# More key chunks summed on VectorE, and a layernorm that divides where v is split, in capped attention followed by a spatial gate

## The chip, the core and the metric

One core of a Trainium2 chip runs the kernel in one launch. The metric is the device time in microseconds (us). TensorE (PE) multiplies matrices, VectorE (DVE) and ScalarE (ACT) work on elements, GpSimd (POOL) does a few integer adds and powers, and SyncE (SP) issues the DMAs.

## The reference

Four batches of twelve heads, 448 positions, head size 64; a model width of 768 and a hidden width of 1024.

```python
scores = cap * np.tanh(scale * (q @ k.T) / cap)
attn = np.exp(scores - max); attn = attn / (np.sum(attn, axis=-1, keepdims=True) + 1e-09)
x = heads side by side of attn @ v                     # (4, 448, 768)
h = gelu_tanh(x @ w_in)                                # (4, 448, 1024)
u, v = h[..., :512], h[..., 512:]
mu = np.mean(v, axis=-1, keepdims=True); var = np.mean((v - mu) ** 2, axis=-1, keepdims=True)
v_n = (v - mu) / np.sqrt(var + 1e-06) * g_ln
v_s = np.einsum('ts,bsd->btd', w_sg, v_n) + b_sg[None, :, None]
return x + (u * v_s) @ w_out
```

## The kernel before

Attention works on two heads (a pair) at a time and on two pairs (a group) together; a batch has three groups, the kernel twelve. The keys of a pair lie in chunks of 128, the last 64 keys of both pairs in one common tail chunk, so a group has seven units: chunks 1 to 3 of either pair and the tail (chunk 0). Per unit there is a score matmul (three products of high and low parts, or one in whole fp32 where PLAIN says so), a tanh and an exp on ScalarE (`tanh`, `exp`, lines 591 and 593), and a value matmul (line 552). The denominators need the sum over all keys of the exponentials. They are made by a matmul with ones (`sum`, line 451), and two units share one such operation. `SUMS` says for each group how much is summed ahead on VectorE (`add`, line 604): with 0 every unit goes to the ones matmul (seven units), with 1 the chunks 2 and 3 are added into chunk 1 of their pair (three units: two pairs and the tail), with 2 the tail is added too, each half of its partitions into its own pair (two units).

After the third group of a batch the denominators go through DRAM, are inverted and come back as rows; the gate of a batch (`gated`) then multiplies x by them, splits x in high and low parts, and multiplies by `w_in` (`hv` for v, line 725, and `hu` for u, line 763), three matmuls for each product. `hv` ends in gelu and layernorm on a tile of 128 positions by 512: statistics, mean, an added epsilon, a power of -0.5 on GpSimd (line 739), centering and scaling in one instruction on VectorE (line 741), then a copy (`v hi`) and a subtraction (`v lo`) that split it. `vsg` (line 780) multiplies by the spatial weights, `bias` and `gate` follow, and `outp` (line 800) multiplies by `w_out`. Matmuls of the gate of one batch run between those of the attention of the next ones.

The weights come as 64-bit floats and are decoded on the chip, 20 pieces of them: a low and a high multiply (lines 376 to 382), a shift, a sign, an integer add on GpSimd (line 396), and a split in high and low (lines 297 and 325). The scaling of q and k (`qk hi`, line 502, and `qk lo`, line 509) splits them likewise.

Nothing is scheduled at run time. Each step is an operation with a number and one or two engines that can do it, and `ORDER` lists them: the number is half of the entry, and an odd entry takes the second engine, which is ScalarE where both are offered. Every engine works through its part of the list in that order, and DMA issues wait in the SP queue in theirs. Buffers are taken from pools when the list comes to an operation: five tiles for exponentials (`p`), two score tiles in PSUM (`sc`).

Of the kernel before, what the change touches and what calls it, by code (L numbers as in the profile page):

```python
# [8 lines left out]
FP32 = mybir.dt.float32  # L9
# [19 lines left out]
SUMS = (0, 1, 1, 1, 0, 1, 1, 1, 2, 2, 2, 2)  # L29
# [87 lines left out]
)  # L117


# [98 lines left out]
def kernel(  # L218
# [13 lines left out]
    nc = tc.nc  # L232
# [668 lines left out]
```

## Time and profile before

| what | value |
|---|---|
| median of 3 runs | 377.6 us (376.75 to 378.32) |
| profiled execution | 376.92 us |
| its span, first to last instruction | 375.1 us |
| busy PE / DVE / ACT / POOL | 370.3 / 301.3 / 211.3 / 40.0 us |

The span lies 1.8 us below the time of its own execution. Matmuls are pipelined and their ends are modelled, so a busy PE can hide a short wait.

### The profile page before, as it was taken

The numbers are of one execution on the slowest core, as the hardware profiler recorded it, in microseconds if no ns is written. First come the engines' busy times: TensorE is split into PE (matmuls) and PEld (weight loads), VectorE is DVE, ScalarE is ACT, GpSimd is POOL, SyncE is SP. The second block draws the span as 40 slices with busy tenths as digits, with TensorE's granted clock in tenths as the row PEclk, the third lists the DMA queues.
The fourth block names the chain that finished last, engine by engine and source line by source line (L and its number), as shares of the span: only waits on it lengthen the run. The fifth ranks groups of instructions, "written<-read, shape, count | busy, mean of one in ns | idle before, by whom it ended". The sixth has DMA issues, their size and how long they took to land.

```text
span 375.1 us, 5508 instructions
## 1 busy us (share of the span) xinstructions
PE 370.3 (99%) x2064; PEld 251.9 (67%) x2064; DVE 301.3 (80%) x559; ACT 211.3 (56%) x275; POOL 40.0 (11%) x39
## 2 busy tenths in 40 slices
PE   9999999999999999999999999999999999999995
PEld 4334343455877497546478976486889999889995
DVE  2799999999999999989894779779276988438763
ACT  5999999995685758697914377751031411033200
POOL 0231121510310312030000100000001000001000
PEclk9999999999999999999999999999999999999999
DMA  7898264454371244146520022202120101400004
GB/s 262 290 285 280 91 187 151 118 158 150 98 255 44 65 135 172 43 134 201 150 80 2 20 73 46 76 3 78 36 74 24 47 5 50 171 2 0 2 0 171
DMA packets 23130, 39.65 MB, mean 106 GB/s; under 512 B 5472, under 2 KB 17728, under 8 KB 23104
## 3 DMA queue, kind: packets, MB, share of 16 engines
q1 hardware_dynamic: 22816, 38.96, 33.0%
q8 instruction: 16, 0.26, 0.3%
q10 hardware_dynamic: 288, 0.34, 0.3%
q14 instruction: 10, 0.08, 0.1%
HBM read 33.28 MB, written 6.02 MB: 105 GB/s over the span
## 4 chain that ended last, share of the span: by engine, by line
PE 96%; DVE 2%; ACT 1%; issue 0%; DVEq 0%; ACTq 0%
PE ps L552 15%; PE ps L725 13%; PE ps L763 13%; PE sc L520 11%; PE ps L800 10%; PE ps L780 9%; PE sc L800 6%; PE den L451 5%; PE sc L528 3%; PE sc L763 3%; PE ps L562 3%; PE sc L725 2%; PE sc L536 2%; PE sc L780 1%; PE ps L352 1%; DVE p L604 1%
## 5 line engine op out<-in xcount | busy, mean ns | idle before, releaser
L593 ACT ACTIVATE p<-p,cap 128x896 f32<-128x896 f32 x84 | 84.8, 1041 | 0.7
L591 ACT ACTIVATE p<-sc 128x896 f32<-128x896 f32 x63 | 56.4, 911 | 15.7 <-PE sc L520 6.9
L552 PE MATMUL ps<-p,v 128*64 128x448 f32 x288 | 61.3, 551 | 0.0
L604 DVE TENSOR_TENSOR p<-p,p 128x896 f32<-128x896 f32 (+1 forms) x48 | 53.8, 1130 | 5.5 <-PE ps L552 3.0
L725 PE MATMUL ps<-win,rg 128*128 128x512 f32 x205 | 50.3, 391 | 0.0
L763 PE MATMUL ps<-rg,win 128*128 128x448 f32 x223 | 50.3, 366 | 0.0
L520 PEld LDWEIGHTS sc<-hl 64*128 64x128 f32 x378 | 32.7, 184 | 25.6 <-ACT p L591 11.7
L520 PE MATMUL sc<-hl 64*128 64x448 f32 x378 | 48.3, 383 | 0.0
L763 PEld LDWEIGHTS ps<-rg,win 128*128 128x128 f32 x223 | 41.8, 188 | 4.4 <-issue 0.7
L725 PEld LDWEIGHTS ps<-win,rg 128*128 128x128 f32 x205 | 38.4, 188 | 8.3 <-issue 0.7
L396 POOL TENSOR_TENSOR stage<-stage 128x512 int32<-128x512 int32 (+1 forms) x20 | 30.6, 1532 | 113.4 <-DVE stage L391 58.1
L552 PEld LDWEIGHTS ps<-p,v 128*64 128x64 f32 x288 | 17.5, 136 | 34.1 <-issue 22.0
L706 ACT ACTIVATE t<-ps 128x448 f32<-128x448 f32 (+1 forms) x25 | 14.2, 567 | 46.4 <-PE ps L725 29.3
L800 PE MATMUL ps<-rg,wout 128*128 128x448 f32 x166 | 39.7, 368 | 0.0
L800 PEld LDWEIGHTS ps<-rg,wout 128*128 128x128 f32 x166 | 30.9, 188 | 5.3 <-issue 2.7
L780 PE MATMUL ps<-wsg,rg 128*128 128x448 f32 x130 | 30.6, 369 | 0.0
L711 ACT ACTIVATE t<-t 128x448 f32<-128x448 f32 (+1 forms) x30 | 18.0, 602 | 20.6 <-DVE t L708 20.6
L739 POOL TENSOR_TENSOR sm<-sm,pw 128x1 f32<-128x1 f32 x14 | 8.7, 627 | 186.7 <-DVE sm L737 177.9
L708 DVE SCALAR_TENSOR_TENSOR t<-t,ps 128x448 f32<-128x448 f32 (+1 forms) x25 | 16.2, 647 | 13.3 <-ACT t L706 13.3
L780 PEld LDWEIGHTS ps<-wsg,rg 128*128 128x128 f32 x130 | 24.0, 188 | 4.1 <-issue 1.0
L800 PE MATMUL sc<-rg,wout 128*128 128x448 f32 x98 | 24.3, 365 | 0.0
L591 ACT ACTIVATE p<-sc,qsc 128x896 f32<-128x896 f32 x21 | 21.0, 1005 | 5.4 <-PE sc L536 1.9
(115 smaller groups left out, 468.2 us busy)
## 6 DMA issues: line engine op xcount, KB each, us to landing
raw<-in_qk_dram SPq DMA_DIRECT2D x22, 448.0 KB
stage<-in_w_in_dram SPq DMA_DIRECT2D x12, 512.0 KB
n<-spread SPq DMA_DIRECT2D x24, 224.0 KB
out_dram<-x SPq DMA_DIRECT2D x23, 224.0 KB
v<-in_vp_dram SPq DMA_DIRECT2D x24, 192.0 KB
stage<-in_w_out_dram SPq DMA_DIRECT2D x8, 384.0 KB
u<-in_w_sgT_dram SPq DMA_DIRECT2D x4, 224.0 KB
vt<-in_vt_dram SPq DMA_DIRECT2D x12, 64.0 KB
```

The lines of the kernel that those rows point to most:

```text
L396: nc.gpsimd.tensor_tensor(out=a.bitcast(I32), in0=a.bitcast(I32), in1=hi, op=ALU.add)
L451: nc.tensor.matmul(out=den.t[32 * j:32 * j + 32, :S], lhsT=ones_sb[:, kind, NP - 1 - kind - p:NP + 31 - kind - p], rhs=src.t[:, h, :], sta ...
L520: nc.tensor.matmul(out=sc.t[:, h, :S], lhsT=hl[s].t[rows, w, 1, 128 * c - 128:128 * c], rhs=hl[s].t[rows, m, 0], start=(k == 0), stop=(k = ...
L552: nc.tensor.matmul(out=pav[s].t[64 * h:64 * h + 64, :S], lhsT=v[s].t[:, 128 * (c - 1) + 64 * h:128 * (c - 1) + 64 * h + 64], rhs=p.t[:, h, ...
L591: op(name("tanh", s, c), "act", c_act(2 * S, True, raw_scores), lambda p=p, sc=sc, r=raw_scores: nc.scalar.activation(out=p.t, in_=sc.t[:, ...
L593: op(name("exp", s, c), "act", c_act(2 * S, False, True), lambda p=p: nc.scalar.activation(out=p.t, in_=p.t, func=ACTF.Exp, scale=cap_sb), ...
L604: op(name("add", s, t), "dve", c_tt(2 * S), lambda: nc.vector.tensor_tensor(out=a.t[rows], in0=a.t[rows], in1=p.t[rows], op=ALU.add), rd=[ ...
L711: op(tag + " tanh", "act", c_act(n), lambda: nc.scalar.activation(out=view(), in_=view(), func=ACTF.Tanh, scale=GELU_C * GELU_A), wr=[sq])
L725: nc.tensor.matmul(out=ps.t[:, :HF], lhsT=(xl if a else xh)[c].t[:, t * 128:t * 128 + 128], rhs=win[w][:, c, HF:], start=(c == 0 and k == ...
L763: nc.tensor.matmul(out=ps.t[:, :S], lhsT=win[w][:, c, f * 128:(f + 1) * 128], rhs=(xl if a else xh)[c].t[:, :S], start=(c == 0 and k == 0) ...
L780: nc.tensor.matmul(out=ps.t[:, :S], lhsT=(vl if a else vh)[c].t[:, f * 128:(f + 1) * 128], rhs=wsg[w][:, c, :], start=(c == 0 and k == 0), ...
L800: nc.tensor.matmul(out=ps.t[:, :S], lhsT=wout[w][:, f, c * 128:(c + 1) * 128], rhs=(gl if a else gh)[f].t[:, :S], start=(f == 0 and k == 0 ...
```

## The change

`SUMS` changes for four groups: the fifth from 0 to 1, the sixth to the eighth from 1 to 2. The layernorm instruction now only centers, with the sign turned, and may run on either engine; it waits for the mean alone. The division by the deviation moves into the copy (a multiply by a column, on either engine) and the subtraction (one instruction that multiplies and subtracts) which split v. The turned sign is taken back by negated gains, `gneg`, one new instruction. The high multiply of the weight decoding may run on ScalarE. `ORDER` is a new one for 1581 operations in place of 1574: ten adds and the negated gains more, four ones matmuls less. In it ten high multiplies, ten scalings of q and k (`qk hi`, which had both engines offered before and ran on VectorE 21 times) and six centerings stand on ScalarE, and the four copies of the spatial weights (`sg hi`), which were on ScalarE, on VectorE.

```diff
-SUMS = (0, 1, 1, 1, 0, 1, 1, 1, 2, 2, 2, 2)
+SUMS = (0, 1, 1, 1, 1, 2, 2, 2, 2, 2, 2, 2)
...
+    gneg = wp.tile([128, KF], FP32, name="gneg")
...
+    op("gneg", "dve", 0.15, lambda: nc.vector.tensor_scalar(
+        out=gneg, in0=g_sb, scalar1=-1.0, scalar2=None, op0=ALU.mult), rd=[k_const], wr=[k_neg])
...
-        def high_bits():
+        def high_bits(e):
             _, hi, a = words()
-            nc.vector.tensor_scalar(out=a, in0=f32(hi), scalar1=2.0 ** -112, scalar2=None, op0=ALU.mult)
+            if e == "dve":
+                nc.vector.tensor_scalar(out=a, in0=f32(hi), scalar1=2.0 ** -112, scalar2=None, op0=ALU.mult)
+            else:
+                nc.scalar.activation(out=a, in_=f32(hi), func=ACTF.Copy, scale=2.0 ** -112)
...
-            op(name("layernorm", t), "dve", 0.55, lambda: nc.vector.tensor_scalar(
-                out=vv(), in0=vv(), scalar1=sm.t[:, 6:7], scalar2=sm.t[:, 0:1],
-                op0=ALU.subtract, op1=ALU.mult), rd=[sm], wr=[v2])
+            def center(e):
+                if e == "dve":
+                    nc.vector.tensor_scalar(
+                        out=vv(), in0=vv(), scalar1=sm.t[:, 6:7], scalar2=-1.0, op0=ALU.subtract, op1=ALU.mult)
+                else:
+                    nc.scalar.activation(out=vv(), in_=vv(), func=ACTF.Identity, scale=-1.0, bias=sm.t[:, 6:7])
+
+            def both(tag, rows, hi, lo, rd, wr_hi, wr_lo):
+                def high(e):
+                    if e == "dve":
+                        nc.vector.tensor_scalar(out=hi(), in0=v2.t[rows, :HF], scalar1=sm.t[rows, 0:1], scalar2=None, op0=ALU.mult)
+                    else:
+                        nc.scalar.activation(out=hi(), in_=v2.t[rows, :HF], func=ACTF.Copy, scale=sm.t[rows, 0:1])
...
+                op("%d v%s lo %d" % (b, *tag), "dve", c_tt(HF) + 0.06, lambda: nc.vector.scalar_tensor_tensor(
+                    out=lo(), in0=v2.t[rows, :HF], scalar=sm.t[rows, 0:1], in1=f32(hi()), op0=ALU.mult, op1=ALU.subtract),
+                   rd=rd + [(sm, "r"), wr_hi], wr=[wr_lo], fast=True)
...
+            op(name("layernorm", t), BOTH, lambda e: 0.55 if e == "dve" else c_act(HF, False, True), center,
+               rd=[(sm, "m")], wr=[v2], fast=True)
...
-                out=tt.t[:, :S], in0=ps.t[:, :S], scalar=g_sb[:, f:f + 1], in1=bsg_sb, op0=ALU.mult, op1=ALU.add),
+                out=tt.t[:, :S], in0=ps.t[:, :S], scalar=gneg[:, f:f + 1], in1=bsg_sb, op0=ALU.mult, op1=ALU.add),
```

## Rows read from the trace of the kernel before

**Rows 1.** The page: busy us (share of the span) xinstructions, and the granted clock.
```profile
PE 370.3 (99%) x2064; PEld 251.9 (67%) x2064; DVE 301.3 (80%) x559; ACT 211.3 (56%) x275; POOL 40.0 (11%) x39
...
PEclk9999999999999999999999999999999999999999
```

**Rows 2.** Windows of 25 us: busy us (xinstructions) of PE, PEld, DVE, ACT, POOL; last GB/s.
```profile
0.00:25.00 25.00, 24.11 (x142) 9.85 (x144) 15.52 (x30) 20.57 (x24) 5.18 (x8) 1.00 0.84 271
25.00:50.00 25.00, 25.00 (x170) 9.66 (x170) 24.38 (x40) 24.16 (x27) 4.08 (x3) 1.00 0.55 184
50.00:75.00 25.00, 24.94 (x184) 10.43 (x179) 24.09 (x35) 23.86 (x27) 8.12 (x5) 1.00 0.54 169
75.00:100.00 25.00, 25.00 (x137) 14.63 (x132) 24.14 (x43) 17.35 (x26) 2.27 (x2) 1.00 0.44 141
100.00:125.00 25.00, 25.00 (x131) 19.37 (x131) 23.84 (x63) 17.67 (x28) 5.13 (x5) 1.00 0.43 129
```

**Rows 3.** Timeline, 52 to 62 us and 175 us: start, length, what, idle before, releaser.
```profile
52.93 1.68 POOL L396 TENSOR_TENSOR stage<-stage 128x512 int32<-128x512 int32 x1 [5.73 <-DVE stage L386]
...
53.37 2.19 DVE L604 TENSOR_TENSOR p<-p,p 128x896 f32<-128x896 f32 x1
...
55.20 1.36 PE L451 MATMUL den<-p,const_sb 128*32 128x448 f32 x8
...
55.65 0.92 ACT L591 ACTIVATE p<-sc 128x896 f32<-128x896 f32 x1 [0.66 <-DVE p L604]
...
58.62 1.09 DVE L604 TENSOR_TENSOR p<-p,p 128x896 f32<-128x896 f32 x1 [0.29 <-PE ps L552]
...
60.16 2.21 DVE L604 TENSOR_TENSOR p<-p,p 128x896 f32<-128x896 f32 x1
...
175.57 0.96 PE L451 MATMUL den<-p,const_sb 128*32 128x448 f32 x8
```

**Rows 4.** The chain that ended last, in order of time: start, us, what.
```profile
21.23 1.64 PE den L451 x16
...
88.72 1.63 PE den L451 x12
```

**Rows 5.** VectorE's groups by form: xcount | busy us, mean ns | idle before, releaser.
```profile
L604 DVE TENSOR_TENSOR p<-p,p 128x896 f32<-128x896 f32 x40 | 45.2, 1139 | 1.0 <-PE ps L552 0.5
...
L502 DVE TENSOR_SCALAR hl<-raw,root 128x832 fp32r<-128x832 f32 x21 | 14.4, 686 | 3.2 <-DMA raw<-in_qk_dram 2.3 <-PE sc L520 0.8
...
L297 DVE COPY x<-ps 128x448 f32<-128x448 f32 x13 | 7.9, 614 | 0.3 <-PE ps L552 0.3
...
L604 DVE TENSOR_TENSOR p<-p,p 64x896 f32<-64x896 f32 x8 | 8.7, 1087 | 4.5 <-PE ps L552 2.6 <-ACT p L593 1.9
...
L741 DVE TENSOR_SCALAR t<-t,sm 128x512 f32<-128x512 f32 x14 | 7.7, 555 | 2.2 <-POOL sm L739 2.1
...
L297 DVE CAST rg<-x 128x448 fp32r<-128x448 f32 x17 | 6.5, 383 | 0.1
...
L382 DVE TENSOR_SCALAR stage<-stage 128x512 f32<-128x512 f32 x12 | 4.9, 418 | 2.9 <-DMA stage<-in_w_in_dram 2.9
...
L325 DVE TENSOR_TENSOR wsg<-u,wsg 128x448 fp32r<-128x448 f32 x4 | 2.5, 615 | 0.0
```

**Rows 6.** ScalarE's groups by form, the same columns.
```profile
L593 ACT ACTIVATE p<-p,cap 128x896 f32<-128x896 f32 x84 | 84.8, 1041 | 0.7
...
L299 ACT ACTIVATE wsg<-u 128x448 fp32r<-128x448 f32 x4 | 2.3, 572 | 0.0
...
L378 ACT ACTIVATE stage<-stage 128x512 int32<-128x512 uint32 x2 | 1.4, 696 | 2.6 <-DMA stage<-in_w_in_dram 2.6
L341 ACT ACT_TABLE_LOAD x1 | 1.3, 1283 | 1.2 <-PEq L887 1.2
```

**Rows 7.** The power on GpSimd, and who waited for it: us, times, longest.
```profile
L739 POOL TENSOR_TENSOR sm<-sm,pw 128x1 f32<-128x1 f32 x14 | 8.7, 627 | 186.7 <-DVE sm L737 177.9 <-DMA n<-spread 8.8
...
DVE t L741 <- POOL sm L739: 2.1, 3, 1.0
```

More of the change, by code (lines that the diff above doesn't have):

```diff
@@ L344 @@
         out=guard, in0=guard, scalar1=1e-9, scalar2=None, op0=ALU.mult), wr=[k_guard])
+    k_neg = Buf()
+    op("gneg", "dve", 0.15, lambda: nc.vector.tensor_scalar(
+        out=gneg, in0=g_sb, scalar1=-1.0, scalar2=None, op0=ALU.mult), rd=[k_const], wr=[k_neg])
     def warm():
@@ L399, in decode @@
            rd=[(st, "w")], wr=[(st, "l")], fast=True)
-        op(tag + "high", "dve", c_ts(n), high_bits, rd=[(st, "w"), (st, "h")], wr=[(st, "a")], fast=True)
+        op(tag + "high", BOTH, lambda e: c_copy(e, n) + (0.045 if e == "act" else 0.0), high_bits, rd=[(st, "w"), (st, "h")], wr=[(st, "a")], fast=True)
         op(tag + "shift", "dve", c_ts(n), shift, wr=[(st, "a")], fast=True)
@@ L734, in hv @@
             sm = Buf(sm_p)
-            op(name("stats", t), "dve", 0.69, lambda: nc.vector.bn_stats(out=sm.t[:, 0:6], in_=vv()), rd=[v2], wr=[sm])
-            op(name("mean", t), "dve", 0.18, lambda: nc.vector.bn_aggr(out=sm.t[:, 6:8], in_=sm.t[:, 0:6]), wr=[sm])
+            op(name("stats", t), "dve", 0.69, lambda: nc.vector.bn_stats(out=sm.t[:, 0:6], in_=vv()), rd=[v2], wr=[(sm, "r")])
+            op(name("mean", t), "dve", 0.18, lambda: nc.vector.bn_aggr(out=sm.t[:, 6:8], in_=sm.t[:, 0:6]),
+               rd=[(sm, "r")], wr=[(sm, "m")])
@@ L737, in hv @@
             op(name("eps", t), "dve", 0.15, lambda: nc.vector.tensor_scalar(
-                out=sm.t[:, 0:1], in0=sm.t[:, 7:8], scalar1=4e-6, scalar2=None, op0=ALU.add), wr=[sm])
+                out=sm.t[:, 0:1], in0=sm.t[:, 7:8], scalar1=4e-6, scalar2=None, op0=ALU.add), rd=[(sm, "m")], wr=[(sm, "r")])
             op(name("power", t), "pool", 0.55, lambda: nc.gpsimd.tensor_tensor(
-                out=sm.t[:, 0:1], in0=sm.t[:, 0:1], in1=pw, op=ALU.pow), rd=[k_pw], wr=[sm], fast=True)
-            op(name("layernorm", t), "dve", 0.55, lambda: nc.vector.tensor_scalar(
-                out=vv(), in0=vv(), scalar1=sm.t[:, 6:7], scalar2=sm.t[:, 0:1],
-                op0=ALU.subtract, op1=ALU.mult), rd=[sm], wr=[v2])
+                out=sm.t[:, 0:1], in0=sm.t[:, 0:1], in1=pw, op=ALU.pow), rd=[k_pw], wr=[(sm, "r")], fast=True)
@@ new lines, in center @@
+            def center(e):
[10 more added lines that the diff above has]
+                        nc.scalar.activation(out=hi(), in_=v2.t[rows, :HF], func=ACTF.Copy, scale=sm.t[rows, 0:1])
+                op("%d v%s hi %d" % (b, *tag), BOTH, lambda e: c_ts(HF) + 0.06 if e == "dve" else c_act(HF, False, True), high,
+                   rd=rd + [(sm, "r")], wr=[wr_hi], fast=True)
+                op("%d v%s lo %d" % (b, *tag), "dve", c_tt(HF) + 0.06, lambda: nc.vector.scalar_tensor_tensor(
+                    out=lo(), in0=v2.t[rows, :HF], scalar=sm.t[rows, 0:1], in1=f32(hi()), op0=ALU.mult, op1=ALU.subtract),
+                   rd=rd + [(sm, "r"), wr_hi], wr=[wr_lo], fast=True)
@@ L744, in hv @@
+            op(name("layernorm", t), BOTH, lambda e: 0.55 if e == "dve" else c_act(HF, False, True), center,
+               rd=[(sm, "m")], wr=[v2], fast=True)
             if t < FC:
                 h, lo = vh[t], vl[t] = Buf(r_p), Buf(r_p)
-                cop(name("v hi", t), lambda: h.t, vv, HF, [v2], [h])
-                sub(name("v lo", t), lambda: lo.t, vv, lambda: f32(h.t), HF, [v2, h], [lo])
+                both(("", t), slice(0, 128), lambda: h.t, lambda: lo.t, [v2], (h, 0), (lo, 0))
@@ L751, in hv @@
                 mine, other = slice(TL * n, TL * n + TL), slice(TL - TL * n, 2 * TL - TL * n)
-                cop(name("v tail hi", n), lambda h=h, m=mine: h.t[m], lambda m=mine: v2.t[m, :HF], HF, [v2], [(h, 0)])
-                sub(name("v tail lo", n), lambda h=h, o=other: h.t[o], lambda m=mine: v2.t[m, :HF],
-                    lambda h=h, m=mine: f32(h.t[m]), HF, [v2, (h, 0)], [(h, 1)])
+                both((" tail", n), mine, lambda h=h, m=mine: h.t[m], lambda h=h, o=other: h.t[o], [v2], (h, 0), (h, 1))
         uu = {}
@@ L785, in vsg @@
             op(name("bias", f), "dve", c_tt(S) + 0.06, lambda: nc.vector.scalar_tensor_tensor(
-                out=tt.t[:, :S], in0=ps.t[:, :S], scalar=g_sb[:, f:f + 1], in1=bsg_sb, op0=ALU.mult, op1=ALU.add),
-               rd=[ps, k_const, k_bsg], wr=[tt])
+                out=tt.t[:, :S], in0=ps.t[:, :S], scalar=gneg[:, f:f + 1], in1=bsg_sb, op0=ALU.mult, op1=ALU.add),
+               rd=[ps, k_neg, k_bsg], wr=[tt])
             op(name("gate", f), "dve", c_tt(S), lambda: nc.vector.tensor_tensor(
```

158 rows, old and new, of the table ORDER are left out of this document.

## The prediction

> **What bounds the kernel now.** I read the page's busy times first, then the windows of 25 us, then the chain that ended last, then the groups of VectorE and ScalarE, and last a piece of the timeline. TensorE is busy 99% of the span, at a granted clock of 1.0 in every slice (the 2.4 GHz level) [rows 1]. The windows say the same stage by stage: from 25 us on TensorE is busy in all of every stretch shown, to within 0.06 us of 25, so its busy time is the time of the kernel, and any matmul taken out shortens it unless a wait takes its place. The same windows show what a wait could come from. VectorE is busy 24.4, 24.1 and 24.1 us of the three stretches from 25 to 100 us, ScalarE 24.2 and 23.9 us of the two from 25 to 75 us and only 17.4 us of the next [rows 2]. So three engines are full until about 75 us, two until about 125 us, and after that TensorE alone is. A modelled end of a matmul can hide a short wait in these busy times; the timeline shows one: at 53.37 an add of VectorE takes 2.19 us, twice what the next one takes (1.09), because GpSimd's integer add began at 52.93; the denominator matmuls that need its sum stretch to 1.36 us, where a later operation of the kind takes 0.96, and ScalarE sits 0.66 us until the same add ends [rows 3].
>
> **The change, part by part.**
>
> *Denominators.* In code 0 a group of two pairs sends seven units to the ones matmul, in code 1 three, in code 2 two, and a matmul operation takes two units. Before, the batches have 13, 13, 8 and 6 units, so 7, 7, 4 and 3 operations, 21. After, 13, 8, 6 and 6 units, so 7, 4, 3 and 3, which is 17. Four operations go, three of them in batch 1. In the chain two whole operations (16 matmul records) take 1.64 us, and a whole with a half one (12 records) 1.63 us, so an operation costs 0.82 us whether it is full or half [rows 4]. 4 x 0.82 = 3.3 us come off TensorE.
>
> *Adds.* The group that goes from code 0 to code 1 gains four adds over 128 partitions, the three groups from 1 to 2 gain two each over 64. 4 x 1.14 + 6 x 1.09 = 11.1 us more on VectorE [rows 5]. None of it lies on TensorE's path while VectorE keeps ahead; without that cover an add costs its 1.1 us.
>
> *What leaves VectorE.* Decoding the order's parity (an odd number takes the second engine), ten of twenty decoding multiplies now run on ScalarE (0.42 us each at most on VectorE), ten of 21 scalings of q and k (0.69), and six of fourteen centerings (0.56); four copies of the spatial weights come back (0.38). That is 4.2 + 6.9 + 3.3 - 1.5 = 12.9 us off, so over the whole span VectorE ends about 2 us lighter than before [rows 5]. On ScalarE a multiply of a strided stage has its nearest row in the low words (0.70), a scaling of 832 columns in the exponential of 896 with a pointer scale (1.04), a centering of 512 in the low words again: at most 10 x 0.70 + 10 x 1.04 + 6 x 0.70 - 4 x 0.57 = 19 us more for an engine that is idle 44% [rows 1, 6]. After 75 us this hides under TensorE. In this trace the strided operation costs 0.70 us there against 0.42 on VectorE, over ten of them 2.8 us, which idle time pays: nothing in the sum [rows 2, 5, 6]. The Trainium skill, ScalarE: Activation LUTs (Rules for kernel authors), puts multiplies on VectorE and speaks against this part; if the difference reached TensorE, the sum would be 2.8 us higher.
>
> *Layernorm.* Centering needs only the mean, so GpSimd's power (0.63 us) leaves the way between mean and centering, and the division goes into the copy and the subtraction that were there anyway. VectorE waited for that power three times, 2.1 us in all [rows 7]. No matmul waited with it, so I take zero for TensorE, and 2.1 us of slack for VectorE as the upper bound. The copy becomes a multiply with a pointer: between the plain cast of 512 columns (0.42) and the two-scalar form (0.56), so at most 14 x 0.14 = 2 us, spread over the four gates. The negated gains are one instruction on four columns, below 0.42 us; it lies in the first stretch, where VectorE is busy 15.5 us of 25 [rows 2, 5].
>
> *New order.* The first eleven operations of TensorE are the same, and the last ones end in the same two halves, so the ramps at both ends are taken as equal. On the SP queue the load of constants now stands behind one more load of q and k (448 KB). The first denominator matmul is its first user; the loads move about 270 GB/s in this stretch [rows 2], so the constants land some 1.7 us later. I take zero; if it is late, it costs below 1.7 us once, when nothing else runs ahead.
>
> *The stall term.* Here the cover is thin. Up to the last value matmul of batch 1's fifth pair ScalarE has three decoding operations more and one copy less: 3 x 0.70 - 0.57 = 1.5 us, and TensorE comes there two sums earlier (1.6 us). Against these 3.1 us stand 2.0 us that ScalarE was idle from 25 to 75 us, so it is short by 1.1 us if it can use all of them and by 3.1 us if none [rows 2, 6]. In VectorE's order, ahead of the first hidden-layer matmul stand four more adds (4.6) and two more pairs of copy and subtraction of spatial weights (2.0), and six operations fewer (five of 0.42 and a PSUM copy of 0.61): 3.9 us more, with TensorE there two sums earlier (1.6), so 5.5 us to find. Its idle time from 25 to 75 us is 1.5 us. The rest, 4.0 us, is there only if adds stretched by GpSimd get rarer: each such stretch costs 1.1 us, and two stand close together at 53 and 60 us [rows 3]. In the new order a copy out of PSUM or the reciprocal follows GpSimd's add at three of the four places between the last group of batch 0 and the second of batch 1, and one of the added adds at the fourth. So the bounds are -0.4 us (the present hold goes, 1.36 - 0.96, and nothing comes) and 4.0 us. I take ScalarE's lower shortage less that hold, 1.1 - 0.4 = 0.7 us: two shortages in one stretch overlap instead of adding up, and the new places of GpSimd's adds are in VectorE's favour.
>
> **The sum.** The profiled execution took 376.9 us (375.1 us of span and 1.8 us around it). 376.9 - 3.3 + 0.7 = 374.3 us; the median of the runs shown is 0.7 us above the profiled execution, so 375.0 us.
>
> **The rivals.**
>
> *ScalarE becomes the bound until 75 us.* For it: it is busy 96% there and gets work. Against: the next stretch has 7.6 us of idle time, so nothing is lost later. Its price lies between 1.1 and 3.1 us; with 2.1 in place of 0.7 it is 376.4 us.
>
> *VectorE becomes the bound (the other side).* The adds come early, the relief (six of the ten multiplies, which decode the output weights, and all scalings) late. If GpSimd stretches as many adds as now, TensorE waits 4.0 us ahead of the first hidden-layer matmuls: 376.9 - 3.3 + 4.0 + 0.7 = 378.3 us, slower than before. It decides from a shortage of 3.3 us on; with two further stretched adds of 1.1 us (6.2) it is 380.5 us.
>
> *Table loads.* The centering on ScalarE uses a function that the trace never shows (Identity). If it were not in the loaded table, each of six would cost a load of 1.28 us there and one back, 15.4 us on ScalarE, of which the three ahead of the first spatial matmul (7.7) could reach TensorE: 375.0 + 7.7 = 382.7 us. For it: nothing in the trace. Against: copy, square, tanh and exponential run under a single load [rows 6]. ScalarE: Activation LUTs in the Trainium skill (Table sets: the hidden batching unit) says that identity is among the cheap functions that every set holds; no run shown has one, and by it this rival falls away.
>
> *The stalls that are there go too.* If the new order also removes the present hold and brings none, 376.9 - 3.3 - 0.4 + 0.7 = 373.9 us.
>
> **How the numbers follow.** A measurement of this kernel tells about 0.5% (1.9 us) from no change: faster means below 375.7, slower above 379.5. The forecast with its own range (stall 0 to 1.4, so 374.3 to 375.7) has 0.5. The rival where stalls go has 0.1, faster too. ScalarE's has 0.2, nearly all of it within 0.5%. VectorE's has 0.18, of which 0.14 within and 0.04 slower. Table loads have 0.02. That makes 0.62 faster, 0.32 same, 0.06 slower. Leaving out the upper part of VectorE's case and the table loads, and the far end below, the range is 373.4 to 377.4.
>
> **What would show each step.** Right: 17 denominator operations (132 records of the ones matmul for 33 units, where 160 stand for 40), TensorE at 99% with a span of about 372.5; 58 adds; ten multiplies and six centerings on ScalarE with one table load in the trace; no wait of VectorE for the power at the centering. Wrong: denominator or hidden-layer matmuls between 30 and 130 us that start where an add or a subtraction of VectorE ends, windows there in which TensorE's records are stretched, VectorE above 24.4 us of 25 (its rival) or ScalarE above 24.2 (its own). The prediction is wrong if TensorE's work is not what sets the time in that part, so that four operations less change who waits and not how long.

## The result, and the profile after

The changed kernel takes 380.81 us (median of 5 runs, 379.21 to 381.24) beside 377.14 us for the kernel before (5 runs): a ratio of 1.0088, 95% interval 1.0058 to 1.0117. That is slower by 3.7 us in the medians, and outside the range that was forecast. The profiled execution took 379.21 us with a span of 377.4 us, 2.3 us more than before. It is the fastest of the five, so the trace below can show 2.3 of the 3.7 us and not the rest.

The page of the changed kernel first: busy times, the granted clock, and the engines' shares of the chain that ended last.

```profile
PE 371.0 (98%) x2036; PEld 249.1 (66%) x2036; DVE 304.1 (81%) x543; ACT 227.6 (60%) x302; POOL 47.2 (12%) x39
...
PEclk9999999999999999999999999999999999999999
...
PE 80%; DVE 10%; ACT 5%; issue 2%; DMA 2%; SPq 0%; DVEq 0%; ACTq 0%
```

TensorE has 28 matmuls less than in [rows 1] and is busy 0.7 us longer. Its share of the chain falls to 80%, where the page of before has 96%; VectorE's rises from 2% to 10%. The two lines of the kernel before, its chain and its ones matmul:

```profile
PE 96%; DVE 2%; ACT 1%; issue 0%; DVEq 0%; ACTq 0%
...
L451 PE MATMUL den<-p,const_sb 128*32 128x448 f32 x160 | 19.9, 550 | 0.0
```

The windows of 25 us, in the columns of [rows 2], say where:

```profile
25.00:50.00 25.00, 24.66 (x166) 9.12 (x166) 24.65 (x38) 24.30 (x29) 5.98 (x3) 1.00 0.48 156
50.00:75.00 25.00, 25.00 (x180) 10.51 (x174) 24.61 (x38) 24.72 (x29) 5.41 (x2) 1.00 0.46 133
75.00:100.00 25.00, 24.54 (x125) 13.62 (x122) 24.54 (x38) 22.62 (x32) 7.58 (x2) 1.00 0.43 145
100.00:125.00 25.00, 24.64 (x127) 18.68 (x127) 24.18 (x63) 16.72 (x29) 4.87 (x5) 1.00 0.46 133
```

VectorE is fuller in all four stretches (24.38, 24.09, 24.14 and 23.84 before, [rows 2]), and TensorE, which was busy to within 0.06 us, has gaps in three. The groups by form (count, busy us and mean ns, idle before) show that the parts of the change are there as they were read:

```profile
L459 PE MATMUL den<-p,const_sb 128*32 128x448 f32 x132 | 16.3, 551 | 0.0
...
L612 DVE TENSOR_TENSOR p<-p,p 128x896 f32<-128x896 f32 x44 | 49.2, 1121 | 2.9 <-ACT p L601 2.2 <-PE ps L560 0.4
...
L612 DVE TENSOR_TENSOR p<-p,p 64x896 f32<-64x896 f32 x14 | 16.9, 1206 | 1.5 <-PE ps L560 0.9
...
L513 ACT ACTIVATE hl<-raw,root 128x832 fp32r<-128x832 f32 x10 | 9.8, 983 | 0.1
...
L755 ACT ACTIVATE t<-t,sm 128x512 f32<-128x512 f32 x6 | 4.3, 720 | 4.1 <-DVE sm L744 4.0
...
L390 ACT ACTIVATE stage<-stage 128x512 f32<-128x512 f32 x4 | 2.7, 680 | 0.0
...
L342 ACT ACT_TABLE_LOAD x1 | 1.3, 1283 | 1.2 <-PEq L912 1.2
...
L404 POOL TENSOR_TENSOR stage<-stage 128x512 int32<-128x512 int32 x12 | 28.2, 2359 | 69.9 <-DVE stage L394 35.8 <-DVE stage L399 34.1
```

The ones matmul has 132 records and 16.3 us in place of 160 and 19.9; 58 adds take 66.1 us; ScalarE has the scalings, the centerings and the multiplies (the row has four, of 512 columns; six more have 384), and still loads one table. The timeline (start, length, what, idle before and releaser) shows what the full VectorE does to the others:

```profile
31.96 1.68 POOL L404 TENSOR_TENSOR stage<-stage 128x512 int32<-128x512 int32 x1 [8.46 <-DVE stage L394]
...
32.40 2.20 DVE L612 TENSOR_TENSOR p<-p,p 128x896 f32<-128x896 f32 x1
...
34.69 0.92 ACT L599 ACTIVATE p<-sc 128x896 f32<-128x896 f32 x1 [0.51 <-DVE p L612]
...
42.32 4.30 POOL L404 TENSOR_TENSOR stage<-stage 128x512 int32<-128x512 int32 x2 [8.67 <-DVE stage L394]
...
45.38 1.53 DVE L298 CAST win<-stage 128x512 fp32r<-128x512 f32 x1
...
75.86 6.18 POOL L404 TENSOR_TENSOR stage<-stage 128x512 int32<-128x512 int32 x1 [11.01 <-DVE stage L394]
...
80.88 2.11 DVE L612 TENSOR_TENSOR p<-p,p 64x896 f32<-64x896 f32 x1
...
83.03 0.92 ACT L599 ACTIVATE p<-sc 128x896 f32<-128x896 f32 x1 [1.22 <-DVE p L612]
...
95.37 1.40 POOL L404 TENSOR_TENSOR stage<-stage 128x512 int32<-128x512 int32 x1 [13.34 <-DVE stage L399]
...
95.52 2.14 DVE L517 SCALAR_TENSOR_TENSOR hl<-raw,root,hl 128x832 fp32r<-128x832 f32 x1
...
100.25 0.19 PEld L788 LDWEIGHTS ps<-r,win 128*128 128x128 f32 x1 [0.20 <-DVE t L721]
...
331.05 2.26 PE L733 MATMUL ps<-win,rg 128*128 128x512 f32 x9
```

The add at 32.40 takes 2.20 us, twice its usual 1.08, while GpSimd's add runs until 33.64; ScalarE's next tanh waits 0.51 us for it, and TensorE for the exponential behind that. The same happens at 80.88 (tanh waits 1.22 us) and at 95.52, and behind the last one the hidden-layer matmul at 100.25 waits for a gelu of VectorE. A measure of these waits that doesn't lean on modelled ends is the distance from the start of one TensorE operation to the next, against the median distance for the same kinds in the trace of before. Summed over the span, what exceeds that median by 60 ns or more at a time is 7.0 us after and 3.7 before; what exceeds it by less is 2.8 us after and 0.5 before; with the distances below the median counted it is 5.7 us more. The medians themselves sum to 3.4 us less, and 5.7 - 3.4 are the 2.3 us of the span. So the spared work is there, and two things eat it: waits (3.3 us), and matmuls that follow each other a little more slowly all over the span (2.2 us; the row at 331.05, below). The split between the two depends on how the matmuls are cut into operations: other ways of counting give about 2.5 us for the waits.

### The profile page after: what moved, and what is told of

It is laid out like the page before. It is cut to its first block, busy times and chain, and to the rows that moved or that the text cites. A ratio compares the mean times of both kernels' runs of the same rounds, so it can differ in the third digit from the quotient of the medians.

```text
span 377.4 us, 5487 instructions
## 1 busy us (share of the span) xinstructions
PE 371.0 (98%) x2036; PEld 249.1 (66%) x2036; DVE 304.1 (81%) x543; ACT 227.6 (60%) x302; POOL 47.2 (12%) x39
## 4 chain that ended last, share of the span: by engine, by line
PE 80%; DVE 10%; ACT 5%; issue 2%; DMA 2%; SPq 0%; DVEq 0%; ACTq 0%
PE ps L560 12%; PE ps L825 10%; PE sc L528 10%; PE ps L788 8%; PE ps L733 8%; PE ps L805 8%; PE sc L825 6%; PE sc L788 4%; PE sc L733 3%; PE den L459 3%; ACT p L599 3%; PE ps L570 2%; DVE p L612 2%; PE sc L536 2%; PE sc L805 2%
## 5 line engine op out<-in xcount | busy, mean ns | idle before, releaser
L612 DVE TENSOR_TENSOR p<-p,p 128x896 f32<-128x896 f32 (+1 forms) x58 | 66.0, 1141 | 4.4 <-ACT p L601 2.2
L560 PE MATMUL ps<-p,v 128*64 128x448 f32 x288 | 62.8, 553 | 0.5 <-ACT p L601 0.5
L404 POOL TENSOR_TENSOR stage<-stage 128x512 int32<-128x512 int32 (+1 forms) x20 | 37.2, 1867 | 114.4 <-DVE stage L399 69.3
L733 PE MATMUL ps<-win,rg 128*128 128x512 f32 x188 | 47.9, 396 | 0.0
L788 PE MATMUL ps<-rg,win 128*128 128x448 f32 x206 | 47.0, 367 | 0.0
L788 PEld LDWEIGHTS ps<-rg,win 128*128 128x128 f32 x206 | 38.5, 188 | 5.0 <-issue 1.4
L733 PEld LDWEIGHTS ps<-win,rg 128*128 128x128 f32 x188 | 35.1, 188 | 8.8 <-issue 1.4
L714 ACT ACTIVATE t<-ps 128x448 f32<-128x448 f32 (+1 forms) x23 | 13.0, 566 | 37.1 <-PE ps L733 25.8
L716 DVE SCALAR_TENSOR_TENSOR t<-t,ps 128x448 f32<-128x448 f32 (+1 forms) x23 | 14.9, 647 | 17.1 <-ACT t L714 17.1
L517 DVE SCALAR_TENSOR_TENSOR hl<-raw,root,hl 128x832 fp32r<-128x832 f32 x21 | 23.5, 1121 | 1.4 <-ACT hl L513 1.4
```

Of the source, the lines that this page charges most:

```text
L404: nc.gpsimd.tensor_tensor(out=a.bitcast(I32), in0=a.bitcast(I32), in1=hi, op=ALU.add)
L517: op(name("qk lo", s), "dve", c_tt(n) + 0.06, lambda: nc.vector.scalar_tensor_tensor(out=used(hl[s].t[:, 1]), in0=used(raw[s].t), scalar=r ...
L560: nc.tensor.matmul(out=pav[s].t[64 * h:64 * h + 64, :S], lhsT=v[s].t[:, 128 * (c - 1) + 64 * h:128 * (c - 1) + 64 * h + 64], rhs=p.t[:, h, ...
L612: op(name("add", s, t), "dve", c_tt(2 * S), lambda: nc.vector.tensor_tensor(out=a.t[rows], in0=a.t[rows], in1=p.t[rows], op=ALU.add), rd=[ ...
L733: nc.tensor.matmul(out=ps.t[:, :HF], lhsT=(xl if a else xh)[c].t[:, t * 128:t * 128 + 128], rhs=win[w][:, c, HF:], start=(c == 0 and k == ...
L788: nc.tensor.matmul(out=ps.t[:, :S], lhsT=win[w][:, c, f * 128:(f + 1) * 128], rhs=(xl if a else xh)[c].t[:, :S], start=(c == 0 and k == 0) ...
```

## The experiments

Ratios are to the kernel before on the same chip; 0.1% is 0.38 us. Where an expectation speaks of theory C, it is VectorE held by GpSimd's adds.

### Matmuls that follow each other more slowly: a tile's place

The new tile `gneg` stands ahead of nearly all data tiles, which thereby lie further in SBUF (by 32 bytes in the expectations; no trace shows an address). The first run declares it last; the others are the kernel before with an unused tile at that place.

```diff
# e1_gneg_last, from the changed kernel
     bsg_sb = wp.tile([128, S], FP32, name="bsg_sb")
-    gneg = wp.tile([128, KF], FP32, name="gneg")
...
     den_p = Pool([pp.tile([128, 512], FP32, name="den")])
+    gneg = wp.tile([128, KF], FP32, name="gneg")
# e2_before_shifted, from the kernel before (e8_before_pad64: [128, 16], 64 bytes)
     bsg_sb = wp.tile([128, S], FP32, name="bsg_sb")
+    gneg = wp.tile([128, KF], FP32, name="gneg")
```

> The changed kernel with the tile of the negated gains declared behind all others, so that every tile lies where it lay before the change; nothing else differs. Theory A (the tile of 32 bytes moves every later tile off its place, and matmuls that read them are issued more slowly): the interval between hv matmuls falls back from 230 to 234 ns to 226, hu from 206 to 202, and the time falls by the 2.2 us counted in the trace, to about 378.5 us (ratio to before 1.003). Theory B (the intervals come from the new order or the chip of that run): intervals and time stay at 380.8 us (ratio 1.009).

> The kernel before with an unused tile of 16 bytes a partition declared where the change declares the negated gains; the instructions are the same. Theory A (placement): hv intervals go from 226 to 230 to 234 ns, hu from 202 to 206, and the time rises by about 2.2 us, ratio 1.006. Theory B (order or chip): no change, ratio 1.000.

> The kernel before with an unused tile of 64 bytes where the second run had one of 32: every later tile lies 64 bytes further, so at a multiple of 64 but no longer of 128. If a multiple of 64 is what the matmuls want, hv stays at 226 ns and hu at 202 and the time at before's (ratio 1.000); if 128, they rise as in the second run (230 to 234, 206; ratio 1.005).

Measured: 1.006 (1.0039 to 1.0081) with gneg last, 1.0054 (1.0034 to 1.0074) for before with the 16 bytes, 0.9999 (0.9989 to 1.0009) with 64 bytes. An unused tile of 16 bytes alone makes the kernel before 2.0 us slower. Runs of matmuls in the gates, late in the timeline of each (before, 16 bytes, 64 bytes, and the changed kernel with gneg last):

```profile
281.99 4.42 PE L763 MATMUL ps<-rg,win 128*128 128x448 f32 x21
...
322.06 3.58 PE L725 MATMUL ps<-win,rg 128*128 128x512 f32 x15
```
```profile
283.12 4.50 PE L764 MATMUL ps<-rg,win 128*128 128x448 f32 x21
...
323.70 3.66 PE L726 MATMUL ps<-win,rg 128*128 128x512 f32 x15
```
```profile
281.79 4.36 PE L764 MATMUL ps<-rg,win 128*128 128x448 f32 x21
...
321.72 3.66 PE L726 MATMUL ps<-win,rg 128*128 128x512 f32 x15
```
```profile
330.86 2.22 PE L734 MATMUL ps<-win,rg 128*128 128x512 f32 x9
```

With 16 bytes 15 `hv` matmuls take 3.66 us in place of 3.58 and 21 `hu` matmuls 4.50 in place of 4.42; with 64 bytes `hv` takes 3.66 too, but `hu` 4.36, so that gain and loss cancel. Counted from each operation's start to the next, the 16 bytes add 1.1 us to `hv`, 0.6 to `hu` and 0.8 to `outp`, and nothing to the value and ones matmuls. The changed kernel has 2.26 us for nine `hv` matmuls (331.05 above) and 2.22 with gneg last. In that run the small excesses fall from 2.8 to 0.9 us, while the waits rise from 7.0 to 8.1, as they would if a faster TensorE reached the same late operations earlier. So the place of the tile costs about 2 us of TensorE's time in the kernel before. In the changed kernel 1.2 us (380.81 - 379.58) are seen, and there the intervals of the two ratios overlap (1.0058 to 1.0117, and 1.0039 to 1.0081). The runs of the changed kernel that follow start from the one with gneg last.

### GpSimd's add cut short

Almost all of GpSimd's integer add is left out: it works on one column in place of 512 or 384.

```diff
-            nc.gpsimd.tensor_tensor(out=a.bitcast(I32), in0=a.bitcast(I32), in1=hi, op=ALU.add)
+            nc.gpsimd.tensor_tensor(out=a[:, :1].bitcast(I32), in0=a[:, :1].bitcast(I32), in1=hi[:, :1], op=ALU.add)
```

> The first run's kernel with GpSimd's integer add cut to one column of 512, so that it leaves out almost all of that add (the decoded weights are wrong). It takes away what stretches VectorE's operations beside GpSimd. Theory C (the new stalls of TensorE between 25 and 150 us come from VectorE, held up by GpSimd's adds): the stalls there fall from 5.6 us to under 2.5, the time falls by 2.5 us or more against the first run's kernel. Theory D (ScalarE sets them): stalls and time fall by less than 1 us.

> The kernel before with the same cut of GpSimd's add (almost all of it left out). It has 1.6 us of stalls behind 25 us, one of 0.5 us beside a stretched add. Theory C: about 0.5 to 1 us off, ratio 0.998, so that between this kernel and the third run's kernel the 3.6 us of the four matmul operations appear (ratio of the two about 0.992). Theory D: no change here either, and the two stay within 1 us of their distance with the full add.

Measured: 0.9942 (0.9921 to 0.9963) for the changed kernel, 0.996 (0.9938 to 0.9983) for before. The holds are worth 4.5 us in the new kernel (1.006 less 0.9942) and 1.5 us in the old one. Yet they hardly grew: VectorE instructions beside GpSimd's add took 8.1 us more than the median of their form before, over 12 instructions, and 10.0 us over 14 after. This fits a new kernel with less idle time to take them, and is not yet shown by these two runs. Without holds it is ahead of before by 0.7 us, where 3.6 were spared (19.9 less 16.3 us of ones matmul).

### One part at a time

The fifth group alone from code 0 to 1 in the order of before (`SUMS` entry and four adds where their exponentials end), the same with GpSimd's add cut, three early decoding multiplies put back on VectorE in the new order, and the layernorm part alone in the order of before (its code and gneg last, six centerings kept on VectorE).

```diff
# e5_one_group, e12_one_group_short_add
-SUMS = (0, 1, 1, 1, 0, 1, 1, 1, 2, 2, 2, 2)
+SUMS = (0, 1, 1, 1, 1, 1, 1, 1, 2, 2, 2, 2)
# e6_early_back: three entries of ORDER to the even number (in 0.0 high, in 1.0 low, in 1.0 high)
-119 ... 133 ... 135
+118 ... 132 ... 134
```

> The kernel before, its own order and placement, with the fifth group alone changed from code 0 to code 1: batch 1 needs five denominator operations in place of seven, four whole adds more stand on VectorE between 58 and 75 us, and nothing is taken off VectorE. Theory C (VectorE is full there, beside GpSimd's adds): the two operations give 1.7 us and the adds take 4 x 1.1 us less the 0.5 to 1 us that VectorE has free there, so TensorE's stalls rise by 2 to 3.5 us and the time ends 0.5 to 2 us above before (ratio 1.001 to 1.005). Theory D (VectorE has room): 1.7 us off, ratio 0.9955.

> Before's order with only the fifth group from code 0 to 1 (382.2 us, 5.2 over before), and GpSimd's integer add cut to one column of 512, so that decoded weights are wrong in the others. Theory C (VectorE's adds are held by GpSimd's): most of the 5.2 us go; before itself with the short add took 376.0, less two denominator operations 374.4, so 374.4 to 376. Theory L (plain load: four adds of 1.14 us more than VectorE has idle there, 24.4 and 24.1 us of 25 busy): the wait of 4.5 us at the third denominator operation stays but for the hold of one or two adds (1.1 us each): 379 to 380.

> The first run's kernel with the three early decoding multiplies that the new order gives to ScalarE back on VectorE, at the same places. Theory C (VectorE is the bound of the first 130 us): 3 x 0.42 us more on a full VectorE, the time rises by about 1 us over the first run's kernel (379.6). Theory D (ScalarE is the bound up to 80 us): 3 x 0.57 us off ScalarE, the time falls by 1 to 1.7 us.

> The kernel before with the layernorm part alone: centering on VectorE, the division in the copy and the subtraction, negated gains (their tile declared last, so that nothing moves); order, engines and sums as before. My prediction's step: nothing for TensorE, ratio 1.000. Rival: the multiply with a pointer in place of a cast (0.48 against 0.42 us) and the subtraction that reads it lengthen VectorE's full stretch at 115 to 135 us, up to 0.5 us, ratio 1.001.

Measured: 1.0134 (1.0108 to 1.016) for the one group, 1.007 (1.0048 to 1.0093) with GpSimd's add cut, 1.0077 (1.0062 to 1.0092) with the multiplies back, 0.9999 (0.9984 to 1.0014) for the layernorm part. The third denominator operation of the one-group kernel in its timeline, and its windows, of 25 us and then of 2 us around that wait:

```profile
74.22 1.08 DVE L612 TENSOR_TENSOR p<-p,p 128x896 f32<-128x896 f32 x1
...
75.36 0.19 PEld L459 LDWEIGHTS den<-p,const_sb 128*32 128x32 f32 x4 [3.60 <-DVE p L612]
75.36 1.71 PE L459 MATMUL den<-p,const_sb 128*32 128x448 f32 x4 [2.79 <-DVE p L612]
```
```profile
50.00:75.00 25.00, 21.82 (x150) 8.79 (x148) 24.53 (x34) 23.96 (x27) 6.74 (x3) 1.00 0.55 165
75.00:100.00 25.00, 24.64 (x132) 12.89 (x133) 23.71 (x40) 14.70 (x20) 3.31 (x2) 0.93 0.46 143
...
72.00:74.00 2.00, 0.57 (x4) 0.00 (x0) 1.97 (x3) 1.89 (x3) 0.00 (x0) 1.00 0.95 236
74.00:76.00 2.00, 0.64 (x2) 0.19 (x4) 2.00 (x4) 1.63 (x2) 0.00 (x0) 0.73 0.40 117
76.00:78.00 2.00, 2.00 (x10) 0.91 (x8) 2.00 (x3) 0.00 (x0) 1.67 (x2) 0.50 0.00 0
78.00:80.00 2.00, 2.00 (x16) 1.14 (x14) 2.00 (x3) 0.92 (x1) 1.64 (x1) 0.91 0.41 109
```

Four adds where VectorE has less than 1 us to spare keep TensorE waiting for the last of them (3.6 us by its weight load, 2.8 by its matmul), although the kernel has two denominator operations less. The time is above what either theory gave (0.9955 to 1.005). Of the 5.1 us 2.4 go with GpSimd's add cut, and 1.5 of these the cut gives to before as well. The rest is load, and with it the lower clock behind the wait: TensorE is granted 0.50 from 76 to 78 us, and with the cut too (0.50 from 74 to 76 us there). How much of the rest is the clock's was not separated. The multiplies say that ScalarE is not the engine that is short before 75 us: with three operations fewer there and three more on VectorE the time does not fall (1.0077 beside 1.006, with overlapping intervals). The layernorm part is neutral.

### The adds taken back in the new order

The changed kernel with gneg last and the SUMS of before (all ten adds), of the fifth group only (four), or of the sixth to eighth (six); the ones matmuls that return stand a few TensorE operations behind the exponentials they need.

```diff
-SUMS = (0, 1, 1, 1, 1, 2, 2, 2, 2, 2, 2, 2)
+SUMS = (0, 1, 1, 1, 0, 1, 1, 1, 2, 2, 2, 2)    # e9_adds_back
+SUMS = (0, 1, 1, 1, 0, 2, 2, 2, 2, 2, 2, 2)    # e10_fifth_back
+SUMS = (0, 1, 1, 1, 1, 1, 1, 1, 2, 2, 2, 2)    # e11_late_back
```

> The changed kernel with gneg last and with SUMS of before: the ten adds go, the four denominator operations come back (3.3 us of TensorE); order, engines, decoding and layernorm stay those of the change. Theory V (the added adds leave VectorE behind, and the stalls are theirs): waits of TensorE fall from 8.1 us to about the 3.7 of before, so 379.6 - 4.4 + 3.3 = 378.5 us, within 1 us of the kernel with gneg last and of before. Theory O (the waits come from the rest of the new order: where decoding, GpSimd's adds and the copies stand): they stay, and the time rises by the whole 3.3 us to 382.9.

> The changed kernel with gneg last, and only the fifth group back from code 1 to code 0: four adds of 1.14 us fewer before 65 us, two denominator operations more (1.6 us). Theory V with the early adds as the cause: the waits between 25 and 75 us (2.7 us with gneg last) fall to about 1, and what is late behind them is earlier too: 379.6 + 1.6 - 1.7 - 1 = 378.5 us. Theory O: 379.6 + 1.6 = 381.2 us.

> The changed kernel with gneg last, and the sixth to eighth group back from code 2 to code 1: six adds of 64 partitions fewer (6.5 us of VectorE, from 60 us on), two denominator operations more (1.6 us). Theory V with the later adds as the cause: the waits between 75 and 150 us (4.0 us with gneg last) fall by 2 us or more: 379 us or below. If the early adds are the cause, or theory O: 381.2 us. Together with the run in which the fifth group goes back and the one in which all go back this tells which adds cost more than they spare.

Measured: 1.0177 (1.0159 to 1.0194), 1.0041 (1.0026 to 1.0056) and 1.0107 (1.0089 to 1.0124). The six late adds pay: without them 1.8 us are lost, about their two operations. The four early ones do not: without them the time is the same within the intervals. All ten together give no clean answer: 1.0177 lies above both theories. One tanh had to stand later in that order, since the buffer for it came free later, TensorE waited 1.46 us for an exponential, and VectorE was idle for much of that stretch:

```profile
75.00:100.00 25.00, 23.14 (x131) 11.74 (x128) 17.27 (x30) 20.98 (x28) 1.91 (x1) 1.00 0.51 164
...
89.02 0.97 PE L569 MATMUL ps<-p,v 128*64 128x448 f32 x4 [1.46 <-ACT p L610]
```

### Holds moved, and late adds in the order of before

Six VectorE entries of ORDER moved ahead (0.3 add 3, 0.2 x, 1.0 x, 2.1 qk lo, sg 2 lo, 0 v lo 1), nothing else; then the late adds on the kernel with the layernorm part alone.

```diff
# e14_before_late_adds, e15_before_sixth
-SUMS = (0, 1, 1, 1, 0, 1, 1, 1, 2, 2, 2, 2)
+SUMS = (0, 1, 1, 1, 0, 2, 2, 2, 2, 2, 2, 2)
+SUMS = (0, 1, 1, 1, 0, 2, 1, 1, 2, 2, 2, 2)
```

> The changed kernel with gneg last (379.6 us, 1.006 of before), and six VectorE instructions moved a few places ahead in its own queue, nothing else: four that stood behind the start of a GpSimd add and were held by it (an add of pair 3, a qk lo, a sg lo, a v lo) now stand ahead of the operation that lets that add start, and two copies out of PSUM take places beside it. Work, engines and GpSimd's adds are the same. Theory H (TensorE waits because GpSimd's add holds VectorE operations that a matmul needs): the waits at 35 (0.5 us), 100 (0.4), 119 (0.3) and 130 us (0.6) go: 377.8 us, a ratio near 1.001. Theory L (VectorE is simply short of time, wherever the holds fall): the sum of VectorE's work stays, and so do the waits, a few operations later: 379.6.

> Before's order with the layernorm of the change (gneg last; that alone ran as long as before), and the sixth to eighth group from code 1 to 2: six adds of 64 partitions more, two denominator operations fewer (1.6 us), the fifth group left at code 0. In the new order these six adds were paid by 1.8 us that they spared. If the price of an add is that of its place, and VectorE has room behind 85 us: 377.1 - 1.6 = 375.5 us, a ratio of 0.996. If VectorE (23.8 us of 25 busy from 100 to 125 us) is too full there for six more: 377 or above.

> As the run before it, but only the sixth group goes from code 1 to 2: two adds more at 75 to 90 us, one denominator operation less (0.8 us). If there is room: 376.3 us, a ratio of 0.998. If the adds hold up what follows (the stretch from 75 to 100 us has VectorE busy 24.1 of 25): 377.1 to 378.

Measured: 1.0047 (1.0031 to 1.0063), 1.0445 (1.0412 to 1.0479) and 1.0053 (1.0036 to 1.007). In the first the timeline shows two of the new neighbours of GpSimd's add:

```profile
33.79 0.62 DVE L307 COPY x<-ps 128x448 f32<-128x448 f32 x1
34.33 1.49 DVE L408 SCALAR_TENSOR_TENSOR stage<-stage 128x512 int32<-128x512 int32 x1
...
98.24 1.36 DVE L654 SCALAR_TENSOR_TENSOR d<-d,guard 64x84 f32<-64x84 f32 x1
```

The copy out of PSUM runs unhindered, and the next operation that reads two tiles of SBUF takes the hold (1.49 for 0.69, 1.36 for 0.29). Held time fell from 11.1 to about 9.5 us, the waits at 35 and 130 us went from 1.1 to 0.2 us, and others grew at 73 and 111 us, from 0.9 to 1.5 us. The interval overlaps that of the start, so moving the holds brought nothing that can be told; by the ratios theory L (1.006) is nearer than theory H (1.001). In the order of before two more adds cost 2.0 us; there a hidden-layer matmul waits 1.28 us for a gelu, where it waits 0.42 us for the same gelu with the layernorm part alone:

```profile
112.43 0.47 PE L794 MATMUL ps<-r,win 128*128 128x448 f32 x1 [1.28 <-DVE u L727]
```

Six adds there cost 16.6 us, but that order is a poor one: three tail adds in a row wait for one exponential with the whole queue of VectorE behind them, and the granted clock falls to 0.95 and 0.93 in the windows from 125 to 175 us. It says nothing on what good places would cost.

### The time of the added adds

Everything of the changed kernel (gneg last) stays in place, and only the ten added adds become short; then GpSimd's add as well; then ScalarE's exponentials in batches 0 and 1.

```diff
 # e16_added_adds_short (e17_both_short: with the cut of GpSimd's add above)
+                    w = 1 if g == 4 or g in (5, 6, 7) and t == 0 else S
                     op(name("add", s, t), "dve", c_tt(2 * S), lambda: nc.vector.tensor_tensor(
-                        out=a.t[rows], in0=a.t[rows], in1=p.t[rows], op=ALU.add),
+                        out=a.t[rows, :, :w], in0=a.t[rows, :, :w], in1=p.t[rows, :, :w], op=ALU.add),
 # e18_exp_short: both cuts, and
+                n = 352 if b < 2 else S
-                    out=p.t, in_=p.t, func=ACTF.Exp, scale=cap_sb), rd=[k_cap], wr=[p])
+                    out=p.t[:, :, :n], in_=p.t[:, :, :n], func=ACTF.Exp, scale=cap_sb), rd=[k_cap], wr=[p])
```

> The changed kernel with gneg last (1.006 of before, 379.4 us beside a before of 377.1), in which the ten added adds work on one column of 448 instead of all, so that the denominators of four groups are wrong; order, engines, the other adds and GpSimd's adds stay. Some 10 us leave VectorE where the change had added them. Theory L (VectorE's load with the ten adds is what TensorE waits for): the waits fall from 8.1 us to about the 3.7 of before, and the kernel keeps the 3.6 us that the change spared: 375 us, a ratio of 0.995. Theory O (the waits come from how the rest of the new order is put, as when the adds were taken back and the waits stayed): 378.5 us or more.

> As the run before it, and GpSimd's integer add cut to one column as well, so that decoded weights are wrong too. With GpSimd's add alone cut the changed kernel took 0.994 of before, 2.7 us more than before itself with that cut (0.996) less the 3.6 us of spared work. Theory L: the ten adds are what is left, and the ratio comes to 0.987 (372.3 us). Theory O: it stays at 0.992 to 0.994 (374 to 375 us), since VectorE is no longer the limit without the holds.

> The run with the ten added adds and GpSimd's adds cut (0.9941 of before, 374.9 us, VectorE busy only 21 to 23 us of 25), and the exponentials of batches 0 and 1 on 704 of their 896 columns, so that these are wrong as well: some 0.2 us less for each of 42 of them on ScalarE, which was busy 24.7 to 24.8 us of 25 from 25 to 100 us there. Theory S (with VectorE relieved, ScalarE holds the new order up, and that is the rest of what the 3.6 us of spared work did not give): waits fall further, 372.3 us, a ratio of 0.987. Theory T (the rest is TensorE's own: intervals of matmuls and short waits at the order's places): 0.994, as before this cut.

Measured: 0.998 (0.9971 to 0.999), 0.9941 (0.9924 to 0.9959) and 0.9935 (0.9919 to 0.9952). Windows of the first (adds short), of the run with GpSimd's add short, and of the last (all three):

```profile
50.00:75.00 25.00, 25.00 (x180) 10.53 (x178) 21.88 (x39) 24.72 (x29) 5.38 (x2) 1.00 0.44 127
75.00:100.00 25.00, 25.00 (x133) 14.60 (x129) 22.83 (x39) 23.95 (x34) 3.00 (x2) 1.00 0.46 151
```
```profile
25.00:50.00 25.00, 25.00 (x169) 9.16 (x168) 21.43 (x34) 24.79 (x30) 1.72 (x3) 1.00 0.47 159
50.00:75.00 25.00, 25.00 (x182) 10.52 (x174) 24.04 (x38) 24.71 (x29) 2.84 (x2) 1.00 0.45 134
75.00:100.00 25.00, 25.00 (x133) 14.81 (x131) 24.53 (x43) 24.86 (x36) 2.62 (x3) 1.00 0.47 147
```
```profile
75.00:100.00 25.00, 25.00 (x131) 14.54 (x131) 22.19 (x41) 23.66 (x36) 1.34 (x3) 1.00 0.46 147
```

With nothing but the time of the ten adds gone, 3.0 us come back (1.006 less 0.998) and TensorE is full again from 50 to 100 us. Cutting GpSimd's add gives 4.5 us, and both together no more than that, so the 0.987 of theory L does not come. The two share one shortage, of VectorE's time: once GpSimd's add is cut, the ten adds cost nothing, and once they are cut, GpSimd's add costs 1.5 us (0.998 less 0.9941), as much as in the kernel before. Shorter exponentials then change nothing, although ScalarE was busy 24.7 to 24.9 us of 25; theory S falls.

## Why the prediction was wrong

**The spared work: right.** 132 records in place of 160, 16.3 us of the ones matmul. In medians of before the matmuls sum to 3.4 us less; the step had 3.3.

**The layernorm and the table: right.** The layernorm part alone ran at 0.9999, and the trace has one table load with six centerings by Identity on ScalarE, so that rival fell. VectorE's wait for the power has gone from the centering, as forecast, but it stands now where v is split (2.0 us, four times):

```profile
DVE rg L760 <- POOL sm L748: 2.0, 4, 0.7
```

**The negated gains cost nothing: wrong.** The instruction is as small as it was read; its tile is what costs. By shifting the data tiles it lengthens the run of nearly every gate matmul, 2.0 us on the kernel before; in the changed one 1.2 us show, within overlapping intervals. The prediction asked what the instruction costs and not what its operand moves.

**The stall term of 0.7 us: wrong, and the larger part.** The mechanism that came true is VectorE's rival, which had 0.18: adds early, relief late, a hold by GpSimd as often as before. Its own figure with two further stretched adds was 380.5 us, and that this lies so near 380.81 is in part luck: the adds cost 3.0 us where that sum had 6.2, and the tile and the work that did not arrive (below) make up the rest. The step that failed is the reasoning that the shortages of ScalarE and VectorE overlap and that the new places of GpSimd's adds are in VectorE's favour. Held time rose from 8.1 to 10.0 us in place of falling, VectorE's busy time rose by 2.8 us (301.3 to 304.1) where the prediction had it about 2 lighter, and the adds' own time reaches TensorE with 3.0 us of their 11. The Trainium skill, GPSIMD Engine Reference (1. Specifications), says that GpSimd shares its way to SBUF with VectorE and contends with VectorE's instructions that run in a two-port mode or have two SBUF inputs; for two inputs the trace agrees (1.08 becomes 2.20 us for an add, 0.62 stays 0.62 for a copy out of PSUM). By that rule counting which instruction follows each of GpSimd's adds was sound. But a copy of 0.62 us covers only part of the hold, and the next instruction takes the rest. That need not be one with two tiles: the cast at 45.38 reads one and takes 1.53 us where 0.42 is usual; in which mode it ran no trace shows.

**ScalarE: right that it is not the bound.** Early multiplies taken from it do not help, nor do shorter exponentials once VectorE is relieved. The sign that the prediction had set for it showed all the same (24.30 and 24.72 us of 25 where it named 24.2), so a nearly full engine alone does not tell the bound.

**What stays open.** With VectorE relieved the new kernel stands at 0.994, 2.2 us below before. Before with GpSimd's add cut, less 3.4 us, would stand at 0.987, so about 2.7 us of the spared work do not arrive even then. Counted from each TensorE operation's start to the next, the run with both cuts spends 3.1 us less on ones matmuls than before with GpSimd's add cut, and 2.4 us more on all others: 0.9 on value matmuls, 0.7 on `hu`, 0.3 on `vsg`, the rest in small amounts, and nearly the same with ScalarE relieved too. So they seem to belong to TensorE's own sequence in the new order, a term that the prediction put at zero when it looked there at the ramps and the constants alone. For the value matmuls the count shows how: one takes 0.80 us when another follows and 0.85 to 0.90 when another kind of matmul does, and 34 of the 72 are followed by another where 40 were before. What makes the others longer was not tried. No complete kernel of this study was faster than the one before; the layernorm part alone equals it.

## What to carry to other kernels

Matmuls taken off the engine that is busy 99% are worth their time only as far as the engine that does their work instead has idle time in the same 25 us; over the whole span VectorE had 20% to spare, and the new kernel still lost 3 us to ten adds. Ask of each new tile where it stands: declared last, a small one moves no other; and compare the length of runs of the same matmul in a stage that the change doesn't touch. When an engine is held by another, look at how much idle time is left to absorb the hold, not only at how often it happens.

## What the runs showed of the hardware that was not expected

- An unused tile of 16 bytes ahead of the data tiles makes runs of the gates' matmuls 2% longer (15 of 128x512 from 3.58 to 3.66 us, 21 of 128x448 from 4.42 to 4.50); one of 64 bytes makes the first longer (3.66) and the second shorter (4.36). Which operand's place decides was not tried.
- GpSimd's add waits for VectorE as VectorE waits for it: 6.18 us for a 128x512 add (75.86) beside a run of nine VectorE instructions of the usual length, six of which read two tiles of SBUF; one took 1.68 us in [rows 3].
- A wait costs more than its length when TensorE's clock falls with it. In the one-group kernel TensorE is busy 0.57 of 2 us and then 0.64 of 2 us around 74 us, and the granted clock goes from 1.00 (2.4 GHz) to 0.50 (the 1.2 GHz level) from 76 to 78 us and is back at 1.00 from 80 us on. In the changed kernel, whose waits are shorter, it stays at 1.00 in every window up to 350 us, so none of its loss in these is the clock's.
